# Decode block backward: the last head's two gradient stores, issued from SyncE in parts of 120 and 8 rows

## The chip, the cores and the metric

One NeuronCore of a Trainium2 chip runs the whole program. The metric is the device time of one execution in microseconds (us). Most of the program's data stay in HBM, and 16 DMA engines carry them to and from the on-chip memory. A DMA can be issued from SyncE (SP), from ScalarE (ACT) or from GpSimd (POOL); each of the three has a queue of its own in the profile (q1, q10 and q0).

## What is computed

The reference is the forward pass of a decode block (one new token, batch 2) and its gradients:

```python
h  = x + attention(layernorm(x), k_cache, v_cache, wq, wo)   # 32 heads, 4096 cached keys, 128 per head
h2 = h + relu(layernorm(h) @ w1) @ w2                        # width 640, hidden 1728
out0 = h2;  gradients for x, k_cache, v_cache, wq, wo, w1, w2 from grad_out
```

The two large outputs are the gradients of the caches, `out_2` (keys) and `out_3` (values), each 2 x 32 x 4096 x 128 in bf16. For each of the 64 pairs of batch and head they are outer products. With p the softmax row of 4096 numbers and d the output gradient of the head, the value gradient is p times d. The key gradient is a second row, the gradient of the scores, times the query. Each of the two is 1 MB per head, so 128 of the 362 MB that the program moves are these stores.

## The kernel before

A tile of a head is laid out with 128 partitions of 32 cache positions each: a partition's row is 32 x 128 bf16, 8 KB in one piece, both in HBM and on chip.

The program has two passes over the 64 heads. The first (`p1_iter`) loads a K and a V tile per head and makes the softmax rows and the attention output. The second (`p2_iter`, `p2_tail`) loads V a second time (tile `Wt`), forms the gradient of the scores on TensorE, and makes two tiles on VectorE:

- `gV`, at the end of `p2_iter(j)`: `outer_half` (line 832) twice, and in the last three heads four of the last columns by ScalarE instead (line 899); then the store to `out_3` from GpSimd's queue (line 900).
- `gK`, at the end of `p2_tail(j)`, which runs within the next head's `p2_iter(j + 1)`, or alone after the last head: `outer_half` twice, then the store to `out_2` from GpSimd's queue (line 851).

So GpSimd issues stores in turn, gK of one head and gV of the next. The last two of all are the gV and the gK of head number 63 (`NP1 - 1`, where `NP1` is 64). The `give` after each store hands the tile's buffer to whatever takes it next, which waits for the store by itself; after the last head nothing takes one.

The loops write out all instructions in order (the schedule is by hand). Background generators are woven in between: weight gradients with stores from ScalarE's queue (`outer_rows`, line 968), and the gradient of x. The latter ends with two stores of 5 rows of 256 bytes each, issued by SyncE (`store_row`, line 653), and `out_0` has gone out earlier by the same lines. SyncE issues all loads, too. In program order its last entries are the load of the last `Wt` tile and the two 5-row stores of the gradient of x; the two stores of the last head follow them in time.

At the program's end SyncE waits for all DMAs, one semaphore after another (line 1288), and then all engines meet twice.

Of the kernel before, what the change touches and what calls it, by code (L numbers as in the profile page):

```python
# [15 lines left out]
def kernel(  # L16
# [20 lines left out]
    nc = tc.nc  # L37
# [36 lines left out]
    def pst(shape, dtype, role, name):  # L74

        k = banks[role].pop(0)
        banks[role].append(k)
        return ps.tile(shape, dtype, tag=f"bank{k}", bufs=1, name=name)
# [11 lines left out]
    def take(tag, shape, name):  # L90
        assert free[tag] > 0, (tag, name)
        free[tag] -= 1
        k = homes[tag].pop(0)
        t = pools[k].tile(shape, BF16, tag=f"big{k}", bufs=1, name=name)
        home_of[id(t)] = (tag, k, t)
        return t
# [9 lines left out]
    def give(t, to=None):  # L106
        tag, k, _ = home_of.pop(id(t))
        to = to or goes_to(tag)
        owned[tag] -= 1
        owned[to] += 1  # L110
        free[to] += 1
        homes[to].append(k)
        given_at[k] = step[0]
# [288 lines left out]
    NP1 = len(pairs)  # L402
# [24 lines left out]
    def pair_transpose(nat, g, dve=False, busy=0):  # L427


        t_ps = pst([128, GT // 2, 128], FP32, "tps", "t_ps")  # L430
        warm(t_ps[:].rearrange("p j k -> p (j k)"), nat, g, busy)
        natf = nat[:].bitcast(FP32)
        for j in range(GT // 2):
            cc = (g * GT) // 2 + j
            nc.tensor.transpose(t_ps[:, j, :], natf[:, 2 * cc:2 * cc + 2, :].rearrange("p c k -> p (c k)"), ident_f[:])  # L435
        t_sb = mats.tile([128, GT // 2, 128], FP32, tag="XT", bufs=4, name="t_sb")
        if dve:
            nc.vector.tensor_copy(out=t_sb[:], in_=t_ps[:])  # L438
        else:
            nc.scalar.copy(out=t_sb[:], in_=t_ps[:])  # L440
        return t_sb

    def pair_matvec(dst, t_sb, g, vecs):
        v = t_sb[:].bitcast(BF16).rearrange("p j (k two) -> p j k two", two=2)
        for j in range(GT // 2):
            sc = g * GT + 2 * j
            for par in range(2):
                nc.tensor.matmul(dst[:, sc:sc + 2], lhsT=v[:, j, :, par], rhs=vecs[:, par, :],  # L448
                                 start=(par == 0), stop=(par == 1))

    def natural(cache, b, h):
        return cache[b, h].rearrange("(p sc) d -> p sc d", sc=NSC)
# [377 lines left out]
    def outer_half(dst, row, colp, k, n=HALF):  # L830
        sl = slice(k * HALF, k * HALF + n)
        nc.vector.tensor_tensor(  # L832
            out=pairs_view(dst[:, sl, :]),
            in0=row.rearrange("p (a two) -> p a two", two=2)[:, None, :, :].to_broadcast([128, n, 64, 2]),
            in1=colp[:, sl, None, :].to_broadcast([128, n, 64, 2]), op=ALU.mult)

    def p2_tail(j):

        p = S2[j]
        bp, hp = turns[j]  # L840
        pair_matvec(p["dp"], p.pop("T3"), 3, gom[:, bp, hp, :, :])
        gsp = small.tile([128, NSC, 2], BF16, tag="gsp", bufs=2, name="gsp")
        nc.vector.scalar_tensor_tensor(
            out=gsp[:], in0=p["dp"][:, :, None].to_broadcast([128, NSC, 2]), scalar=negdot[:, hp, bp:bp + 1],
            in1=P_bf[:, p_slot[(bp, hp)], :, None].to_broadcast([128, NSC, 2]), op0=ALU.add, op1=ALU.mult)
        yield
        gK = take("g", [128, NSC, 128], "gK")
        outer_half(gK, p["rb"][:, 128:256], gsp, 0)
        yield
        outer_half(gK, p["rb"][:, 128:256], gsp, 1)  # L850
        nc.gpsimd.dma_start(out=natural(out_2, bp, hp), in_=gK[:])  # L851
        give(gK)
        del S2[j]
        yield
# [3 lines left out]
    def p2_iter(j, nsb):  # L858

        tail = p2_tail(j - 1) if j - 1 in S2 and "T3" in S2[j - 1] else iter(())  # L860
        c = S2[j]
        next(tail, None)
        b, h = turns[j]
        go = gom[:, b, h, :, :]
        bank = pst([128, 512], FP32, "sps", "dp_ps")
        for k, col in enumerate((goc, qsc)):
            nc.tensor.matmul(bank[:, 128 + k * 128:256 + k * 128],  # L867
                             lhsT=col[:, h, b:b + 1].to_broadcast([128, 128]), rhs=ident_bf[:],
                             start=True, stop=True)
        c["dp"] = bank[:, 0:NSC]  # L870
        rb = mats.tile([128, 256], BF16, tag="rb", bufs=3, name="rb")
        nc.scalar.activation(out=rb[:], in_=bank[:, 128:384], func=ACT.Copy, scale=rt[:, b, h:h + 1])  # L872
        pp = small.tile([128, NSC, 2], BF16, tag="pp", bufs=2, name="pp")
        nc.gpsimd.tensor_copy(out=pp[:], in_=P_bf[:, p_slot[(b, h)], :, None].to_broadcast([128, NSC, 2]))
        if nsb:
            pf = small.tile([128, NSB], FP32, tag="pf", bufs=2, name="pf")
            nc.gpsimd.tensor_copy(out=pf[:, 0:nsb], in_=P_bf[:, p_slot[(b, h)], NSC - nsb:NSC])
        c.update(rb=rb, pp=pp)
        c["T0"] = pair_transpose(c["W"], 0)
        next(tail, None)  # L880
        yield
        for _ in tail:
            yield
        c["T1"] = pair_transpose(c["W"], 1)
        pair_matvec(c["dp"], c.pop("T0"), 0, go)
        yield
        c["T2"] = pair_transpose(c["W"], 2)
        pair_matvec(c["dp"], c.pop("T1"), 1, go)
        yield
        c["T3"] = pair_transpose(c["W"], 3)  # L890
        give(c["W"], "g" if j < H and j != 1 and owned["g"] < 3 else None)
        pair_matvec(c["dp"], c.pop("T2"), 2, go)
        gV = take("g", [128, NSC, 128], "gV")
        outer_half(gV, c["rb"][:, 0:128], c["pp"], 0)
        yield
        outer_half(gV, c["rb"][:, 0:128], c["pp"], 1, HALF - nsb)
        if nsb:
            for k in range(nsb):
                nc.scalar.activation(out=gV[:, NSC - nsb + k, :], in_=rb[:, 0:128], func=ACT.Copy, scale=pf[:, k:k + 1])
        nc.gpsimd.dma_start(out=natural(out_3, b, h), in_=gV[:])  # L900
        give(gV)
        yield

# [266 lines left out]
    for n, (i, j) in enumerate(plan):  # L1170
# [22 lines left out]
        if j is not None:  # L1193
            if j < NP1:
                bg_until(("go", *turns[j]))
            nsb = 0 if i is not None else NSB if j < H and fin is None else NSB // 2 if j >= NP1 - 3 else 0
            g2 = p2_iter(j, nsb) if j < NP1 else p2_tail(NP1 - 1)
        elif open_tail:
            g2 = p2_tail(open_tail[0])
# [93 lines left out]
```

## Time and profile before

| what | value |
|---|---|
| time, median of three runs | 898.54 us (893.46 to 898.84) |
| the profiled execution | 896.3 us, of which 894.4 us span |
| moved over DMA | 361.84 MB, mean 405 GB/s |
| TensorE busy, share of the span | 83% |
| VectorE busy | 77% |
| GpSimd's queue (q0) | 134.23 MB, 36.1% of 16 engines' time |
| SyncE's queue (q1) | 211.13 MB, 58.1% |
| last gV store issued / landed | 876.05 / 890.29 us |
| last gK store issued / landed | 878.33 / 892.72 us |

The span runs from the first to the last instruction of the program; the time contains it and some 2 us around it. Times of day in this text are microseconds from the span's start. A store is issued by an instruction of half a microsecond on its engine; its data move later, when the DMA engines get to it, and the last of its 16 landings (one per DMA engine) ends it.

### The profile page before, as it was taken

What the parts mean: (1) busy time and instruction counts of PE and PEld (TensorE: products, weight loads), DVE (VectorE), ACT (ScalarE), POOL (GpSimd) and SP (SyncE); (2) the same over time, 40 slices, a digit from 0 to 9 for tenths busy, and PEclk for the clock granted to TensorE, in tenths of its full rate; (3) what the DMA queues carried; (4) which work ended last, traced back from release to release, by engine and by line L of the source; (5) the groups of instructions that cost most, each with busy time, mean ns of one, the idle gap of its engine ahead of it and who ended that gap; (6) DMA issues with size and microseconds to landing.
All of it is one profiled execution on the core that took longest, in us unless ns stands there. A gap on an engine that the chain in (4) does not pass through costs nothing.

```text
span 894.4 us, 24636 instructions
## 1 busy us (share of the span) xinstructions
PE 740.6 (83%) x10145; PEld 622.7 (70%) x10145; DVE 688.1 (77%) x1283; ACT 469.5 (52%) x1184; POOL 198.6 (22%) x342
## 2 busy tenths in 40 slices
PE   4999899999998998897867887875698988858881
PEld 4887788888887887777757776764566765635570
DVE  2666778976888897796678897877988468898992
ACT  1344334443555665464545776553476666537751
POOL 1344434442210000000011231111222111111141
PEclk9999989999999999898995555555657566555655
DMA  9999999999979999999999999999999999999996
GB/s 377 420 412 403 409 407 418 411 414 410 356 299 366 422 422 424 422 422 423 414 382 390 416 416 418 414 412 422 398 394 423 426 421 424 423 426 424 423 423 256
DMA packets 56304, 361.84 MB, mean 405 GB/s; under 512 B 5696, under 2 KB 11904, under 8 KB 15488
## 3 DMA queue, kind: packets, MB, share of 16 engines
q1 hardware_dynamic: 34536, 211.13, 58.1%
q0 software_dynamic: 18432, 134.23, 36.1%
q10 hardware_dynamic: 3224, 14.92, 4.0%
q8 instruction: 80, 1.31, 0.6%
q14 instruction: 32, 0.26, 0.1%
HBM read 211.11 MB, written 149.13 MB: 403 GB/s over the span
## 4 chain that ended last, share of the span: by engine, by line
DMA 37%; PE 31%; DVE 19%; issue 6%; ACT 3%; POOL 1%; SPq 0%; POOLq 0%; DVEq 0%; ACTq 0%
DMA out_dram<-gK 16%; PE t_ps L435 13%; DMA Vt<-in_A_v_cache_dram 12%; PE m_ps L469 7%; DMA out_dram<-gV 5%; DVE gV L832 5%; DVE gK L832 4%; DVE rows L658 4%; PE s_ps L448 3%; DVE pk L476 3%; DMA wo_t<-in_A_wo_dram 2%; PE u_ps L498 2%; DMA Kt<-in_A_k_cache_dram 2%; PE dp_ps L448 2%; ACT t_sb L440 1%
## 5 line engine op out<-in xcount | busy, mean ns | idle before, releaser
L440 ACT COPY t_sb<-t_ps 128x512 f32<-128x512 f32 x479 | 272.6, 587 | 181.3 <-PE t_ps L435 177.0
L448 PEld LDWEIGHTS <-t_sb 128*128 128x128 bf16 x4096 | 169.7, 103 | 75.1 <-ACT t_sb L440 33.3
L435 PE MATMUL t_ps<-ident_f,Wt 128*128 128x128 f32 x832 | 200.0, 392 | 0.4 <-ACT t_sb L440 0.4
L476 DVE TENSOR_TENSOR pk<-Kt,ep 128x2048 bf16<-128x2048 bf16 x128 | 156.3, 1222 | 44.7 <-ACT ep L523 26.0
L469 PE MATMUL m_ps<-pk,Vt 128*128 128x129 bf16 x2048 | 175.8, 224 | 15.0 <-DMA Vt<-in_A_v_cache_dram 14.4
L832 DVE TENSOR_TENSOR gK<-rb,gsp 128x2048 bf16<-128x2048 bf16 x128 | 153.4, 1224 | 18.5 <-DMA out_dram<-gV 16.9
L832 DVE TENSOR_TENSOR gV<-rb,pp 128x2048 bf16<-128x2048 bf16 (+2 forms) x128 | 147.1, 1172 | 23.6 <-DMA out_dram<-gK 23.1
L435 PEld LDWEIGHTS t_ps<-ident_f,Wt 128*128 128x128 f32 x832 | 140.2, 204 | 32.1 <-issue 26.5
L435 PE MATMUL t_ps<-ident_f,Kt 128*128 128x128 f32 x1024 | 153.4, 285 | 3.7 <-DMA Kt<-in_A_k_cache_dram 3.5
L469 PEld LDWEIGHTS <-Vt 128*128 128x128 bf16 x2048 | 130.9, 100 | 18.1 <-DMA Vt<-in_A_v_cache_dram 16.1
L435 PEld LDWEIGHTS t_ps<-ident_f,Kt 128*128 128x128 f32 x1024 | 116.3, 148 | 5.1 <-issue 2.6
L486 POOL COPY pk<-ep 128x16 bf16<-128x16 bf16 x80 | 83.6, 1047 | 152.3 <-ACT ep L523 107.0
L448 PE MATMUL dp_ps<-gom,t_sb 128*128 128x2 bf16 x2048 | 96.0, 168 | 14.5 <-ACT t_sb L440 14.1
L900 POOL DMA_DIRECT2D out_dram<-gV x64 | 34.3, 536 | 317.7 <-DVE gV L832 115.6
L448 PE MATMUL s_ps<-gom,t_sb 128*128 128x2 bf16 x2048 | 80.2, 164 | 1.2 <-DVE t_sb L438 1.2
L851 POOL DMA_DIRECT2D out_dram<-gK x64 | 34.1, 533 | 200.3 <-DVE gK L832 149.6
L582 ACT CAST MT<-m_ps 128x128 bf16<-128x128 f32 x64 | 17.0, 266 | 116.3 <-PE m_ps L469 116.3
L965 ACT CAST ot<-o_ps 128x512 bf16<-128x512 f32 (+3 forms) x152 | 66.8, 494 | 8.9 <-DMA out_dram<-ot 7.3
L872 ACT ACTIVATE rb<-dp_ps,rt 128x256 bf16<-128x256 f32 x64 | 30.3, 474 | 45.5 <-PE dp_ps L867 43.2
L658 DVE CUSTOM_DVE_ANT_0 rows<-wo_t,rows 128x640 bf16<-128x640 bf16 x64 | 52.3, 818 | 0.2
L658 DVE CUSTOM_DVE_ANT_0 rows<-wqs,gqr 128x1024 bf16<-128x1024 bf16 x40 | 48.8, 1220 | 0.2
L658 DVE CUSTOM_DVE_ANT_0 rows<-w_t,rows 128x640 bf16<-128x640 bf16 (+2 forms) x58 | 45.9, 792 | 2.8 <-ACT rows L636 2.1
(194 smaller groups left out, 715.7 us busy)
## 6 DMA issues: line engine op xcount, KB each, us to landing
Kt<-in_A_k_cache_dram SPq DMA_DIRECT2D x64, 1024.0 KB, 16.5
Vt<-in_A_v_cache_dram SPq DMA_DIRECT2D x64, 1024.0 KB, 16.6
out_dram<-gV POOLq DMA_DIRECT2D x64, 1024.0 KB, 14.1
out_dram<-gK POOLq DMA_DIRECT2D x64, 1024.0 KB, 14.3
Wt<-in_A_v_cache_dram SPq DMA_DIRECT2D x52, 1024.0 KB, 11.4
out_dram<-ot ACTq DMA_DIRECT2D x6, 960.0 KB, 12.7
wq_t<-in_A_wq_dram SPq DMA_DIRECT2D x5, 1024.0 KB, 11.0
wqs<-in_A_wq_dram SPq DMA_DIRECT2D x5, 1024.0 KB, 22.2
```

What stands on the lines that cost most here:

```text
L435: nc.tensor.transpose(t_ps[:, j, :], natf[:, 2 * cc:2 * cc + 2, :].rearrange("p c k -> p (c k)"), ident_f[:])
L440: nc.scalar.copy(out=t_sb[:], in_=t_ps[:])
L448: nc.tensor.matmul(dst[:, sc:sc + 2], lhsT=v[:, j, :, par], rhs=vecs[:, par, :], start=(par == 0), stop=(par == 1))
L469: nc.tensor.matmul(r["m"][:, 0:129], lhsT=r["V"][:, sc, :], rhs=r["pk"][sc // HALF][:, sc % HALF, 0:129], start=(sc == 0), stop=(sc == NSC ...
L476: nc.vector.tensor_tensor(out=p["pk"][k][:, :, 0:128].rearrange("p s (a two) -> p s a two", two=2), in0=p["K"][:, sl, :].rearrange("p s (a ...
L486: nc.gpsimd.tensor_copy(out=col, in_=e)
L658: nc.vector.tensor_tensor_reduce(out=junk[0:kc, 0:width], in0=in0, in1=in1, scale=1.0, scalar=0.0, op0=ALU.mult, op1=ALU.add, accum_out=acc)
L832: nc.vector.tensor_tensor(out=pairs_view(dst[:, sl, :]), in0=row.rearrange("p (a two) -> p a two", two=2)[:, None, :, :].to_broadcast([128 ...
L851: nc.gpsimd.dma_start(out=natural(out_2, bp, hp), in_=gK[:])
L872: nc.scalar.activation(out=rb[:], in_=bank[:, 128:384], func=ACT.Copy, scale=rt[:, b, h:h + 1])
L900: nc.gpsimd.dma_start(out=natural(out_3, b, h), in_=gV[:])
L965: nc.scalar.copy(out=ot[0:P, k, n0:n0 + nn], in_=o_ps[0:P, 0:nn])
```

## The change

A new function `store` takes over both stores of the second pass. For all heads but the last it issues what was issued before, from GpSimd. For the last head it issues two DMAs from SyncE: rows 0 to 119, and rows 120 to 127. Data, layout, the order of the computation and all other DMAs stay as they are. SyncE's list of instructions gets four DMAs at its end, behind the two 5-row stores (gV 120, gV 8, gK 120, gK 8 rows); GpSimd's list loses its last two.

```diff
+    def store(dst, t, last):
+
+        if not last:
+            nc.gpsimd.dma_start(out=dst, in_=t[:])
+            return
+        for rows in (slice(0, 120), slice(120, 128)):
+            nc.sync.dma_start(out=dst[rows], in_=t[rows])
+
     def p2_tail(j):
...
         outer_half(gK, p["rb"][:, 128:256], gsp, 1)
-        nc.gpsimd.dma_start(out=natural(out_2, bp, hp), in_=gK[:])
+        store(natural(out_2, bp, hp), gK, j == NP1 - 1)
         give(gK)
...
-        nc.gpsimd.dma_start(out=natural(out_3, b, h), in_=gV[:])
+        store(natural(out_3, b, h), gV, j == NP1 - 1)
         give(gV)
```

## The prediction

> **What bounds the kernel now.** The edit sits in the last 20 us, so I read first what limits that stretch, in the view of windows. The columns after each window are its length, the busy time of the five engines, the granted TensorE clock, the mean busy share of the core's 16 DMA engines, and GB/s.
>
> ```profile
> core 0: us, PE busy (x) PEld busy (x) DVE busy (x) ACT busy (x) POOL busy (x), PEclk, DMA share, GB/s
> 840.00:860.00 20.00, 16.71 (x137) 12.17 (x137) 19.69 (x35) 11.19 (x23) 4.29 (x7) 0.50 1.02 424
> 876.00:884.00 8.00, 0.00 (x0) 0.00 (x0) 2.03 (x2) 0.00 (x0) 1.07 (x2) 0.50 1.00 419
> 884.00:886.00 2.00, 0.00 (x0) 0.00 (x0) 0.00 (x0) 0.00 (x0) 0.00 (x0) 0.50 0.54 229
> 886.00:888.00 2.00, 0.00 (x0) 0.00 (x0) 0.00 (x0) 0.00 (x0) 0.00 (x0) 0.50 0.17 70
> 888.00:890.00 2.00, 0.00 (x0) 0.00 (x0) 0.00 (x0) 0.00 (x0) 0.00 (x0) 0.50 0.08 33
> 890.00:892.00 2.00, 0.00 (x0) 0.00 (x0) 0.00 (x0) 0.00 (x0) 0.00 (x0) 0.50 0.07 29
> ```
>
> DMA is full while data are left, and compute is over at 878 us. Then the share falls to 0.07 and stays there: one engine of 16 is 0.0625. So for the last 4 us a single DMA engine works through what it still owes, and the kernel waits for it. Who waits shows in the timeline of POOL and SP and in SP's waits (waiter, what for, total us, times, longest):
>
> ```profile
> 873.70 0.53 POOL L851 DMA_DIRECT2D out_dram<-gK  x1 [0.25 <-DVE gK L832]
> 876.05 0.53 POOL L900 DMA_DIRECT2D out_dram<-gV  x1 [1.82 <-ACT gV L899]
> 878.33 0.53 POOL L851 DMA_DIRECT2D out_dram<-gK  x1 [1.75 <-DVE gK L832]
> ...
> 867.46 3.63 SPq L653 DMA_DIRECT2D out_dram<-rows  x2
> ...
> SPq L1288 <- DMA out_dram<-gV: 19.2, 1, 19.2
> SPq L1288 <- DMA out_dram<-gK: 2.4, 1, 2.4
> ```
>
> The two stores that the edit touches are issued at 876.05 and 878.33. SP has nothing after its second row store at 870.8, and waits at the program's end for exactly these two.
>
> The trace also has every landing (16 per full transfer, one per DMA engine) and every DMA packet (queue, start, duration, size, not which engine). The last gV store lands on fifteen engines from 881.2 to 886.25 and on the sixteenth at 890.29. The last gK store: fifteen by 888.70, the sixteenth at 892.72. The ten POOL stores before them show the same picture, a last landing 4.0 to 4.6 us after the second last. Meanwhile ACT's large stores land on all 16 within 0.0 to 0.4 us of the second last. So one engine is late by some 4 us in POOL's backlog, and the tail of the windows is that engine. One row of 8 KB costs an engine 0.306 us (packets of 0.309 us, each starting 0.003 us before its predecessor's end), so the eight rows that it has of a 128-row store take 2.45 us.
>
> **The change part by part.** *Taken away:* two issues of 0.53 us on POOL. They end at 876.58 and 878.86. The late engine then works on earlier stores until 887.39, and the engine that finishes first (883.29) is also still on earlier ones, until 878.38. Backlog hides the issue everywhere: saving it is worth 0, from 0 to 0.1.
>
> *Added:* four issues on SP, at 0.29 us (the row stores) to 0.37 us (a Wt load) each. They stand behind the two row stores of L653, the last of which issues at 870.8, before gV is complete at about 876. Both wait for the same DVE and ACT results as before. Nothing stands behind them but the program's end. gK's second part issues about 0.7 us after 878.3, still under the same backlog. Cost 0; without that cover it would be 0.4 to 0.7 us.
>
> *Moved:* 256 rows of 8 KB from queue q0 to q1. Bytes and time per packet stay: 840 to 860 us, with two queues mixed, ran at 424 GB/s against 419 with q0 alone. An engine that holds packets of two queues takes turns between them (in the trace, 256-byte packets of q1 stand between 8 KB packets of q0 without a gap). It then finishes when the sum of its work is done, whatever the order.
>
> What counts is therefore **how many rows the late engine gets**. Before it had 8 + 8. No DMA of 120 or of 8 rows is in the trace. The nearest are the 5-row stores of L653. I strung the packets on one engine together by their starts (a start 3 or 4 ns before the end of the packet ahead). For the last pair, issued at 867.46 and 870.80, the strings are clear: the five 256-byte packets of a store lie on five different engines, and the late engine is one of them. It carries a row at 871.11 and one at 874.40, in the string whose POOL stores complete at 872.42, 875.07, 877.57 and so on to 892.30. (For the pair issued near 800 the strings cross and I can't tell.) So small transfers are dealt row by row, and the late engine is among the first to get one. 120 rows go evenly onto 15 engines in eights. An engine that is served when only five are should be among the fifteen, and among the eight that take one row each of the 8-row part.
>
> That gives 9 + 9 rows, two more than before: 2 x 0.306 = **+0.61 us**. Bounds: 0 + 0 rows (left out of all four parts), at which the second-latest engine ends the kernel, -4.0 us; and 16 + 16 rows (the whole 8-row part on this one engine), +4.9 us. I take 9 + 9, since the 5-row stores are nearest. An end 0.3 us earlier is possible if POOL's last drain, which holds the end until 893.66 (SP is done at 893.36), has less to wait for; but q0's last rows on the late engine take turns with q1's, so I count 0.
>
> The Trainium skill's page "DMA: Bandwidth & Descriptors" (section "Why a DMA increments its semaphore by 16 and not by 1") says that SP's path takes the largest engine count up to 16 that divides the rows, lowest-numbered engines first: 15 for 120 rows, 8 for 8 rows, 5 for 5. By it the late engine, one of five, stays served by all four parts, and the sum would again be +0.61 us; the trace agrees for 5 rows (five packets on five engines), and shows neither 120 nor 8.
>
> Sum: 0 + 0 + 0 + 0.61 = +0.6 us. On the profiled execution (896.3 us, of which 894.4 are span) that is 896.9. The median of the runs is 898.54, 2.2 us above the profiled one, so on it the forecast is **899.1 us**, 0.07% more. About 1% (9 us) is what a measurement of this kernel can tell from no change, so this counts as none.
>
> **The rivals.** *The late engine is the one left out (faster).* If 120 rows go onto fifteen engines, one gets nothing, and if the 8 rows avoid it too, its 16 rows (4.9 us) are gone; it would end at 887.39. The kernel then ends with the second-latest engine, landing at 888.70, or 889.31 if that one gets two single rows: 3.4 to 4.0 us earlier, 894.5 to 895.1 on the median. For it: the tail is exactly one engine, and leaving out one engine is what a 120-row part can do. Against it: that engine took a row of both 5-row stores of the last pair. The same page (section "Latency and other measured facts") notes that engines 7 and 15 are usually the slow ones; if the late one were 15, this rival would hold, at the 894.5 to 895.1 just worked out. The trace bears out one clearly late engine but not its number.
>
> *The small part piles up (slower).* If a part's rows are dealt in blocks of eight, as the 120 are, the 8-row part lands whole on one engine. If that is the late one, it has 16 rows of each store instead of 8: 16 x 0.306 = 4.9 us more, 903.4 on the median. On any other engine it costs at most 4.9 - 4.0 = 0.9 us, since the second-latest has 4.0 us in hand. It decides only if block and late engine meet. Against it: the 5-row stores went onto five engines.
>
> *The late engine gets eights but no single rows:* 0 us, 898.5. This lies inside the forecast's own range.
>
> **How the numbers follow.** The forecast with the 0 us variant: 0.62. Late engine left out: 0.28. Pile-up: 0.10. The three runs spread from 893.46 to 898.84, wider than any of these effects. The forecast's own range is 896 to 900.5 (898.5 to 899.1, and half the spread of the runs downward, some 1.5 upward); the left-out case reaches down to 894.5, and a median that falls low to about 893. The pile-up, at 903 or more, is left outside. Range 893.2 to 900.8. All cases lie within 9 us of 898.5, so only scatter gives the outer classes: faster by over 1% 0.03 (from the left-out case), slower by over 1% 0.02 (from the pile-up), within 1% 0.95.
>
> **What would show it.** Right: the windows of the new profile end with a stretch of some 4 us at a share of 0.06 to 0.08, the last landings of the two 120-row parts are fifteen with one some 4 us behind, and each 8-row part has one late landing too. The SP rows show four issues at L843 of about 0.3 us, after the two row stores. POOL's last store is gK of the head before. Wrong in favour of the left-out case: the share falls from 0.5 to 0 within some 4 us with no one-engine tail, and the wait at the end is for an earlier POOL store or for an engine with little lag. Wrong in favour of the pile-up: the tail at one engine grows from about 4 to about 9 us. The forecast fails altogether if the wait before the end moves to SP's own issue, or if engines stand idle between 878 and 884, which would mean that backlog doesn't hide the four issues.

## The result, and the profile after

The changed kernel takes 898.62 us (median of 22 runs, 894.82 to 900.64). Beside it, the kernel before takes 896.34 us (22 runs, 893.46 to 899.05). The ratio is 1.002 with a 95% interval of 1.001 to 1.0029: about 1.8 us more (0.9 to 2.6). The forecast was 0.61 us more, so its direction holds and its size is too small. That the forecast time of 899.1 us lies so near the measured 898.62 is luck: it was added to the median of the first three runs of the kernel before (898.54), and added to the median of its 22 runs it would be 896.95, some 1.7 us too low.

The profiled execution of the changed kernel took 900.58 us, 898.8 of them span. It is some 4 us behind the one shown of before already ahead of the first change (the second row store is issued at 874.7 us and not at 870.8), which is scatter between executions. So times of day can't be set side by side, only distances. The view of windows at the end of the changed kernel:

```profile
core 0: us, PE busy (x) PEld busy (x) DVE busy (x) ACT busy (x) POOL busy (x), PEclk, DMA share, GB/s
880.00:882.00 2.00, 0.00 (x0) 0.00 (x0) 1.93 (x2) 0.00 (x0) 0.00 (x0) 0.50 1.05 426
882.00:884.00 2.00, 0.00 (x0) 0.00 (x0) 0.00 (x0) 0.00 (x0) 0.00 (x0) 0.50 1.00 299
884.00:886.00 2.00, 0.00 (x0) 0.00 (x0) 0.00 (x0) 0.00 (x0) 0.00 (x0) 0.50 0.90 287
886.00:888.00 2.00, 0.00 (x0) 0.00 (x0) 0.00 (x0) 0.00 (x0) 0.00 (x0) 0.50 0.92 307
888.00:890.00 2.00, 0.00 (x0) 0.00 (x0) 0.00 (x0) 0.00 (x0) 0.00 (x0) 0.50 0.67 254
890.00:892.00 2.00, 0.00 (x0) 0.00 (x0) 0.00 (x0) 0.00 (x0) 0.00 (x0) 0.50 0.26 107
892.00:894.00 2.00, 0.00 (x0) 0.00 (x0) 0.00 (x0) 0.00 (x0) 0.00 (x0) 0.50 0.11 45
894.00:896.00 2.00, 0.00 (x0) 0.00 (x0) 0.00 (x0) 0.00 (x0) 0.00 (x0) 0.50 0.07 29
896.00:898.80 2.80, 0.00 (x0) 0.00 (x0) 0.00 (x0) 0.00 (x0) 0.00 (x0) 0.50 0.01 6
```

Read the last two columns together. At 880 us a full share still moves 426 GB/s. From 882 the share is 1.00 and the rate is 299: the engines are as busy as before and move 30% less. The kernel before has no such rows; it goes from a share of 1.00 at 419 GB/s straight to idle engines. After that the old picture returns: a share of 0.07, one engine of sixteen, until the end. The four issues are in the timeline of SP, and their durations (least, median, most in ns) in the view of line 843:

```profile
871.39 3.63 SPq L653 DMA_DIRECT2D out_dram<-rows  x2
879.76 1.85 SPq L843 DMA_DIRECT2D out_dram<-gV  x2
881.96 3.77 SPq L843 DMA_DIRECT2D out_dram<-gK  x2
```

```profile
L843 SPq DMA_DIRECT2D out_dram<-gV x2: 329/900/1470, 879.8 to 880.1; - x2
L843 SPq DMA_DIRECT2D out_dram<-gK x2: 1737/1864/1992, 882.0 to 884.0; - x2
```

They stand behind the two row stores, as foreseen, but three of them last 1.5 to 2.0 us and not 0.3. In the timeline of POOL the last store is gK of the head before (first fence). SP's wait at the end lasts 11.4 us, from about 885.7, when its own last issue is over (second fence, from the view of waits):

```profile
877.63 0.53 POOL L840 DMA_DIRECT2D out_dram<-gK  x1 [0.25 <-DVE gK L832]
```

```profile
SPq L1296 <- DMA out_dram<-gK: 11.4, 1, 11.4
```

The packet records give the rest. A 120-row part has 15 landings and one early increment of its semaphore; an 8-row part has 8 landings, the other 8 increments coming at once. Strung together backwards from the last packet, the late engine has in each store eight rows of the 120-row part and one row of the 8-row part. From 888.92 to 896.82 it works without a gap and takes turns between the two queues; the eight rows of the large gK part start from 889.24 to 893.75, its row of the small part at 894.37, and the last packets are GpSimd's gK of the head before. Not all of its rows last 0.309 us: from 883.65 on they are 0.59 us longer in all, 0.34 of it in a single row of 0.651 us. And the 256 moved rows last 0.384 us on the mean: the median is still 0.309, but 15.6% take over 0.5 us, the longest 1.405. The last 512 rows of the program, taken alike in both kernels, last 0.312 us before and 0.363 after, which over 16 engines is 512 x 0.051 / 16 = 1.6 us.

### The profile page after: what moved, and what is told of

Its sections match the earlier page's. It is cut to its first block, busy times and chain, and to the rows that moved or that the text cites. A ratio compares the mean times of both kernels' runs of the same rounds, so it can differ in the third digit from the quotient of the medians.

```text
span 898.8 us, 24639 instructions
## 1 busy us (share of the span) xinstructions
PE 744.1 (83%) x10145; PEld 624.6 (69%) x10145; DVE 688.5 (77%) x1283; ACT 469.6 (52%) x1184; POOL 195.6 (22%) x340
## 4 chain that ended last, share of the span: by engine, by line
PE 38%; DMA 32%; DVE 18%; ACT 5%; issue 4%; SPq 1%; DVEq 0%; POOL 0%; ACTq 0%; POOLq 0%
PE t_ps L435 17%; DMA Vt<-in_A_v_cache_dram 12%; DMA out_dram<-gV 8%; PE m_ps L469 7%; DMA out_dram<-gK 5%; DVE gK L832 4%; DVE gV L832 4%; DVE rows L658 4%; PE s_ps L448 3%; DVE pk L476 3%; DMA wqs<-in_A_wq_dram 3%; PE o_ps L967 3%; DMA wo_t<-in_A_wo_dram 2%; ACT t_sb L440 2%; PE u_ps L498 2%
## 5 line engine op out<-in xcount | busy, mean ns | idle before, releaser
L435 PE MATMUL t_ps<-ident_f,Wt 128*128 128x128 f32 x832 | 203.3, 397 | 0.5 <-ACT t_sb L440 0.4
L435 PEld LDWEIGHTS t_ps<-ident_f,Wt 128*128 128x128 f32 x832 | 142.3, 207 | 32.5 <-issue 26.2
```

## The experiments

Two theories stood at first. *Rows*: the late engine has 9 + 9 rows and not 8 + 8, and each row more costs 0.306 us at the end. *Queue*: SyncE's queue, with its neighbours and its place, is what costs. Later a third came up, *dealing*: parts that don't have 128 rows are dealt to the engines in another way, in which the engines hold each other up. Edits are shown against the loop of the changed kernel, unless the text says otherwise. Ratios are to the kernel before, run beside it on the same chip.

**Whole stores from SyncE.** Only the queue changes, nothing is divided.

```diff
-        for rows in (slice(0, 120), slice(120, 128)):
-            nc.sync.dma_start(out=dst[rows], in_=t[rows])
+        nc.sync.dma_start(out=dst, in_=t[:])
```

> The last head's two stores go out from SyncE as before in the change, but whole: 128 rows in one DMA each. Theory A (what the change costs is the two extra rows on the late DMA engine, and slower packets because 120 rows are dealt to the engines in other eights than 128 rows): 8 + 8 rows on the late engine as before, packets of the two stores back at 0.31 us (0.384 us in the change), so the time is that of before within 0.5 us (ratio 1.000). Theory B (the cost is the queue: q1 beside q0 in the last 20 us slows packets): packets stay at 0.36 to 0.40 us, and 0.8 to 1.5 us of the cost stay (ratio 1.001 to 1.0015).

Measured: 896.05 against 896.92 us, ratio 0.9992 (0.9978 to 1.0006). The moved rows last 0.311 us. The issues in SP's timeline:

```profile
876.33 0.35 SPq L842 DMA_DIRECT2D out_dram<-gV  x1
878.79 0.35 SPq L842 DMA_DIRECT2D out_dram<-gK  x1
```

Both the slow rows and the long issues are gone. The queue alone costs nothing that can be measured; the division does.

**The same parts from GpSimd.** Only the division, on the old queue.

```diff
-            nc.sync.dma_start(out=dst[rows], in_=t[rows])
+            nc.gpsimd.dma_start(out=dst[rows], in_=t[rows])
```

> The same parts of 120 and of 8 rows, but issued from GpSimd, as the stores of all other heads. Theory A: if GpSimd deals as SyncE does, the late engine gets 9 + 9 rows and the packets are slow again, +0.6 to +1.8 us over before; if GpSimd deals the 8-row part to other engines than the late one, 8 + 8 rows and 0 to +1 us. Theory B (the queue): everything in one queue, packets at 0.31 us, at most +0.6 us.

Measured: 900.34 against 896.92 us, ratio 1.0039 (1.0024 to 1.0054), 3.5 us more (2.2 to 4.8). That is more than either theory allowed (1.8 us at most). GpSimd's rows in the last 20 us last 0.377 us on the mean. Two engines are late here, not one; the windows of its tail show two sixteenths:

```profile
888.00:890.00 2.00, 0.00 (x0) 0.00 (x0) 0.00 (x0) 0.00 (x0) 0.00 (x0) 0.50 0.15 57
890.00:892.00 2.00, 0.00 (x0) 0.00 (x0) 0.00 (x0) 0.00 (x0) 0.00 (x0) 0.50 0.13 49
892.00:894.00 2.00, 0.00 (x0) 0.00 (x0) 0.00 (x0) 0.00 (x0) 0.00 (x0) 0.50 0.11 45
```

So the slow rows aren't a matter of SyncE's queue, nor of its long issues: POOL issued each part in about half a microsecond. SyncE's queue may be the cheaper one for the divided stores; with one head the two intervals still touch (1.0010 to 1.0029 from SyncE). Why GpSimd's parts cost more than was expected stays open.

**Parts of 125 and 3 rows.** A strong dose of rows: 125 rows should go onto five engines, 25 on each.

```diff
-        for rows in (slice(0, 120), slice(120, 128)):
+        for rows in (slice(0, 125), slice(125, 128)):
```

> Parts of 125 and of 3 rows from SyncE. 125 rows should be dealt to five engines, 25 rows each, 3 rows to three. Theory A (the late engine is among the lowest-numbered five, whichever part is issued): the late engine gets 25 or 26 rows a store instead of 8, 34 to 36 more in all, x 0.306 = +10.4 to +11.0 us, and the tail of one engine lasts some 6 us longer than the other four that got as much. Rival (the late engine is not in the set that a part of 120 or 125 rows starts with): it loses its 16 rows and the five others gain 34 rows less their lead of 4 us: +6.4 us or less, and the five end together.

Measured: 906.25 us, ratio 1.0102 (1.0085 to 1.0118), 9.1 us more. The windows show five sixteenths (0.31) until the end nears, then the late ones:

```profile
886.00:888.00 2.00, 0.00 (x0) 0.00 (x0) 0.00 (x0) 0.00 (x0) 0.00 (x0) 0.50 0.31 127
...
894.00:896.00 2.00, 0.00 (x0) 0.00 (x0) 0.00 (x0) 0.00 (x0) 0.00 (x0) 0.50 0.31 127
...
900.00:902.00 2.00, 0.00 (x0) 0.00 (x0) 0.00 (x0) 0.00 (x0) 0.00 (x0) 0.50 0.09 37
```

The large gK part lands on five engines at 897.01, 897.53, 897.76, 901.06 and 902.58 us, and the last of the three single rows at 902.90. The engine that is late in GpSimd's backlog (its last row there lands at 894.38) is among the five: its 25 rows of the large gK part last until 901.06, and it has no single row. The engine that ends the kernel, with 25 + 1 rows, is the second-latest in GpSimd's backlog (892.03). So rows on the late engines do cost at the end. The forecast was 10.4 to 11.0 us, from 25 or 26 rows on the late engine; 9.1 us (7.6 to 10.6) reaches into it.

**Where the late engine stands.** The kernel before, with its last row stores divided (5 rows as 2 + 3, then as 4 + 1), so that each 256-byte packet marks an engine. The data stored are the same.

```diff
-    def store_row(col_bf, n, dst):
+    def store_row(col_bf, n, dst, first=0):
...
-        nc.sync.dma_start(out=dst, in_=r[0:n])
+        for rows in ([slice(0, first), slice(first, n)] if first else [slice(0, n)]):
+            nc.sync.dma_start(out=dst[rows], in_=r[rows])
...
-            store_row(gxo[:], ND, out_1[b].rearrange("s (c p) -> (s c) p", p=128))
+            store_row(gxo[:], ND, out_1[b].rearrange("s (c p) -> (s c) p", p=128), 2 + 2 * b)
```

> The kernel before, except that the two 5-row stores of the gradient of x go out in parts: 2 and 3 rows the first time, 4 and 1 the second. This marks the engines: the engine that is first in the dealing gets a 256-byte packet of the 2-row, of the 3-row and of the 4-row part; so does the second; the third only of the 3- and the 4-row part; the fourth of the 4-row part; the fifth of none. Where the late engine's string of packets carries them tells its place. No effect on the time is expected (two more issues of 0.3 us on SyncE that nothing waits for).

One execution, 896.0 us. The late engine is known by its landings, the last of each GpSimd store: 870.08, 872.70, 875.30, 877.84 us and so on. Its string of packets, followed along them from 869.56 to 892.07, carries none of the ten marks (870.10 to 875.39), so it isn't among the four engines that these parts used. **The same marks in the changed kernel:**

> The changed kernel with the marks of the run before (2 and 3 rows, then 4 and 1, instead of two times 5), to see in one run the late engine's place and how many rows of the four parts it gets: 9 + 9 if it is among the first eight, 8 + 8 if it is the ninth to fifteenth, 0 + 0 if it is the sixteenth, in which case the tail of one engine is missing and the end comes some 4 us earlier.

One execution, 894.9 us. Here, too, the late engine's string, followed along its landings (870.98, 873.66, 876.17, 878.65 us), carries none of the ten marks. So in both it comes behind the first four in the dealing, while in the kernel before it carries a row of both 5-row stores. The fifth place fits every execution that was read, the one with 125 rows included (one of five, with no row of the 3-row part); a place that changes from one execution to the next isn't shown. A division that gives less to that place wasn't tried.

For the tail I take the distance from the last landing of the gV store of head number 61, which all these kernels issue alike and ahead of the two stores in question, to the last landing of all: 12.21 us before, 12.21 in the marked kernel before, 12.18 with whole stores from SyncE, 13.01 in the changed kernel and 12.83 in the marked changed one. The strings say what it consists of. In the marked changed kernel the late engine has 9 + 9 rows, all of 0.309 to 0.313 us: the two extra rows alone, 0.61 us, as forecast. In the changed kernel it has 9 + 9 as well, but one of the 18 lies ahead of that landing; the distance grows by one row (0.31) and by the 0.59 us that its rows are longer. So there the late engine has 0.61 + 0.59 = 1.2 us more in all, and 0.6 in the marked one: between these two executions, what the slow rows cost differs by whether they fall on the late engine.

**Parts of 112 and 16 rows.** Each engine gets 7 + 1, no engine more than before. If the extra rows are all that costs, the cost is gone.

```diff
-        for rows in (slice(0, 120), slice(120, 128)):
+        for rows in (slice(0, 112), slice(112, 128)):
```

> The parts from SyncE are of 112 and of 16 rows. Both divide by 16, so every engine gets 7 + 1 rows of a store: the late engine has 8 + 8 as before, not 9 + 9. Theory 'rows' (the change's cost is the two extra rows on the late engine): ratio to before 1.000, packets don't matter. Theory 'dealing' (the cost is that parts other than 128 rows are dealt to the engines in pieces of adjacent partitions, so that two engines read through one port at once): packets of the two stores stay slow, 0.35 to 0.42 us on the mean with some near 0.61 (twice 0.306), and 0.5 to 2 us are left (ratio 1.0005 to 1.002).

Measured: 899.1 against 896.5 us, ratio 1.0026 (1.0008 to 1.0043). The cost stays with even rows, and the rows last 0.399 us. Its windows show full shares at falling rates, as in the changed kernel:

```profile
880.00:882.00 2.00, 0.00 (x0) 0.00 (x0) 0.00 (x0) 0.00 (x0) 0.00 (x0) 0.50 0.98 328
882.00:884.00 2.00, 0.00 (x0) 0.00 (x0) 0.00 (x0) 0.00 (x0) 0.00 (x0) 0.50 0.97 283
```

The tail of its profiled execution is the old 12.21 us, though; that execution, at 895.88 us, was the quickest of its twelve, and so shows where the cost isn't rather than where it is.

**Two halves of 64 rows.** As above, with `slice(0, 64), slice(64, 128)`.

> The parts from SyncE are of 64 and 64 rows, 4 rows for each engine, so again 8 + 8 rows a head's store on the late engine. Theory 'dealing': partitions 0 to 63 lie behind half of the ports, so all 16 engines read two to a port and packets go to 0.45 to 0.61 us on the mean while only one part is moving; +1.5 to +4.9 us (ratio 1.0015 to 1.0055). Theory 'rows': even dealing, 0.31 us packets, ratio 1.000.

Measured: 897.83 us, ratio 1.0015 (0.9999 to 1.0031): not told apart from none. The rows are the slowest of all at 0.433 us, 27% of them over 0.5 us. So for one head the cost isn't seen to grow with the mean row. The Trainium skill's page "DMA: Bandwidth & Descriptors" (section "Rules for kernel authors") advises against two transfers to disjoint halves of the partitions, because both go over the same engines. The trace agrees on the engines (16 landings for each half of gV), and adds that rows get slower on the mean.

**Six heads whole from SyncE.** For the lag of the late engine: if GpSimd's queue makes it, moving the last six heads off that queue should take it away. The condition becomes `j >= NP1 - 6`, the store is whole.

> The stores of the last six heads (twelve DMAs) go out whole from SyncE's queue, and only those before them from GpSimd's. Nothing else of SyncE's stands behind them but the four small row stores among them. Theory 'POOL' (the lag of 4 to 6 us of one engine is made by GpSimd's path, for SyncE's and ScalarE's transfers land on all engines within 0.4 us): the lag is not renewed over the last 45 us, the end comes 2 to 4 us earlier (ratio 0.9955 to 0.998). Theory 'engine' (the engine has that much more work, or loses time whatever the queue): the lag moves into SyncE's stores, ratio 1.000.

Measured: 895.99 us, ratio 0.9987 (0.9971 to 1.0003). Three engines now end last within 1.1 us of each other (893.21, 893.73 and 894.26), the other thirteen by 891.47. But the kernel isn't clearly faster, and the idle time has moved:

```profile
860.00:880.00 20.00, 12.12 (x118) 10.40 (x119) 13.74 (x25) 8.43 (x21) 1.73 (x4) 0.50 0.81 335
880.00:890.00 10.00, 3.39 (x44) 2.85 (x42) 6.91 (x7) 3.45 (x8) 0.00 (x0) 0.67 1.01 416
```

DVE is busy 13.74 of 20 us here against 17.85 in the kernel before, the DMA share falls to 0.81, and the last gK tile is done at 886.94 us and not at 878.03. So the lag is smaller at the end, and idle time stands ahead of it instead. Whether GpSimd's queue makes the lag isn't settled by this: three engines stay late in stores that all come from SyncE, but they may have brought that lag along from GpSimd's stores.

**Six heads in parts, and a control.** One head costs 0.2 to 0.3%, close to what can be told. Six should cost six times as much if the dealing is at fault. The control also divides each store in two on SyncE's queue, but by columns, so that every part has 128 rows (of 4 KB). Both keep the condition `j >= NP1 - 6`; the diff leads from the parts of 112 and 16 rows to the control.

```diff
-        for rows in (slice(0, 112), slice(112, 128)):
-            nc.sync.dma_start(out=dst[rows], in_=t[rows])
+        for c in (slice(0, 16), slice(16, 32)):
+            nc.sync.dma_start(out=dst[:, c], in_=t[:, c])
```

> The stores of the last six heads go out from SyncE, each in parts of 112 and 16 rows (8 rows for every engine). Against whole stores of six heads (0.9987 of before) this has the same rows per engine. Theory 'dealing': packets of these stores at 0.38 to 0.42 us instead of 0.31; 12 stores x 8 rows x 0.08 us = up to 7.7 us more for each engine, of which waits in the stretch hide some: +2 to +8 us against the whole stores (ratio to before 1.001 to 1.008), and more than the column halves of this call. Theory 'rows': no more than the column halves, both at 0.9987 to 1.000.

> The control for the last: the same number of DMAs of the last six heads from SyncE, but each part has all 128 rows and half of the columns (4 KB a row), so the rows are dealt as for whole stores. It carries what two DMAs a store cost by themselves (issues, a ring of eight semaphores, a packet more per row). Both theories: packets of 4 KB at 0.155 to 0.16 us, ratio 0.9985 to 1.001.

Measured: by rows 906.02 us against 897.36, ratio 1.0100 (1.0080 to 1.0121); by columns 895.9 us, ratio 0.9987 (0.9974 to 1.0000). This is the reading that decides. The window of 860 to 880 us, parts of rows first, halves of columns second:

```profile
860.00:880.00 20.00, 7.66 (x81) 6.13 (x79) 9.37 (x16) 4.93 (x11) 0.37 (x2) 0.59 0.91 276
```

```profile
860.00:880.00 20.00, 12.36 (x143) 10.47 (x142) 16.81 (x24) 10.58 (x25) 1.73 (x4) 0.59 0.92 370
```

From 860 to 880 us the engines are busy for the same share, 0.91 and 0.92, and move 276 and 370 GB/s. DVE does 9.37 us of work and 16.81. Its waits for buffers whose stores haven't landed yet (from the view of waits, 840 to 910 us: total us, times, longest) are 10.5 us by rows and 3.1 by columns:

```profile
DVE gV L832 <- DMA out_dram<-gK: 6.8, 1, 6.8
DVE gK L832 <- DMA out_dram<-gV: 3.7, 1, 3.7
```

```profile
DVE gV L832 <- DMA out_dram<-gK: 2.6, 1, 2.6
DVE gK L832 <- DMA out_dram<-gV: 0.5, 1, 0.5
```

The same in the queue totals (packets, MB, share of 16 engines' span), in the same order:

```profile
q1 hardware_dynamic: 36456, 223.71, 61.9%
```

```profile
q1 hardware_dynamic: 37992, 223.71, 61.6%
```

The same bytes take 0.619 x 905.3 = 560.4 us of the engines' time by rows and 0.616 x 894.0 = 550.7 by columns, 9.7 us more. The times differ by (1.0100 - 0.9987) x 897 = 10.1 us, or 1.7 us for each of the six heads. That is near what the change costs for its one head (1.8), but it comes by way of buffers that later tiles wait for, and after the last head nothing takes a buffer. So the two sizes need not have the same account.

**Six heads of 120 and 8.** The dealing and the extra rows together.

> The parts of the change, 120 and 8 rows, for the stores of the last six heads, from SyncE. Theory 'rows and dealing' together: as the 112 and 16 rows of this call, and on top 12 x 0.306 = 3.7 us for the first eight engines, which get 9 rows of each store: +0.2 to +0.4% over the 112 and 16 rows if the late engine is among the first eight, as it was where it could be told; 0 if not, and then the sixteenth engine has 96 rows less.

Measured: 906.49 us, ratio 1.0113 (1.0091 to 1.0134). It lies 0.0013 above the even parts, with intervals that overlap: what the uneven rows add over six heads can't be told from nothing here.

**Six heads of 112 and 16 from GpSimd.** The six heads of 112 and 16 rows again, with `nc.gpsimd` in the loop. From SyncE the issues had grown as well, to medians of 1.4 and 1.7 us where columns and whole stores take 0.33. GpSimd's issues don't grow.

> The stores of the last six heads in parts of 112 and 16 rows, as in the run before that cost 1.0% this way, but issued from GpSimd's queue. In that run SyncE's issues of the parts had also grown, to medians of 1.4 and 1.7 us (columns and whole stores: 0.33 us). Theory packets (the cost lies within the DMA engines, whoever issues): the moved rows again last 0.37 us or more on the mean instead of 0.311, and 1536 rows x 0.06 to 0.10 us / 16 engines = 6 to 10 us, a ratio of 1.006 to 1.012. Rival issue (the cost was SyncE's long issues, which brought the stores out late and with them the buffers that VectorE waits for): GpSimd issues in about 0.53 us and idles for most of this stretch, so the ratio goes back to between 0.998 and 1.003, whatever single packets last. A value between 1.003 and 1.006 would mean that both have a part.

Measured: 909.59 against 897.0 us, ratio 1.0149 (1.0126 to 1.0173). The issues (ns) and the same window:

```profile
L843 POOL DMA_DIRECT2D out_dram<-gV x12: 499/518/542, 847.8 to 888.2; - x12
L843 POOL DMA_DIRECT2D out_dram<-gK x12: 499/517/543, 852.8 to 892.4; - x12
```

```profile
860.00:880.00 20.00, 12.33 (x131) 10.29 (x129) 14.29 (x25) 9.29 (x21) 5.84 (x14) 0.59 0.91 283
```

The issues are short, the rows last 0.42 us (those from GpSimd between 860 and 880), and a share of 0.91 again moves only 283 GB/s. So SyncE's long issues aren't the cause. The 4.4 us above the same parts from SyncE ((1.0149 - 1.0100) x 897) fall outside the range that was expected. GpSimd here also waits 19.3 us in all for earlier stores to land before it issues (13.8 for gK, 5.5 for gV), which may be part of it; that wasn't tried by itself.

## Why the prediction was right, and where not

- *Issue on GpSimd, saved: 0.* Right, as far as it can be seen: whole stores from SyncE give 0.9992, an interval that holds 1.
- *Added: four issues of 0.29 to 0.37 us, hidden.* The size is wrong: 0.33, 1.47, 1.74 and 1.99 us. They cost nothing that can be seen: the last one ends at 885.7, 11 us ahead of the end, the DMA share is 0.90 or more to 888 us, and the same division from GpSimd, without long issues, costs no less.
- *Moved: "Bytes and time per packet stay".* This is the step that failed. The bytes stay, the time per row does not: 0.384 us instead of 0.309. Over 256 rows and 16 engines that is 256 x 0.075 / 16 = 1.2 us on the mean engine, a term that the sum has at 0. On the late engine, which sets the end, it was 0.59 us (GpSimd's rows included) in the profiled execution and nothing in the marked one. The rows of 424 and 419 GB/s that I argued from compare queues; they say nothing of parts with other than 128 rows. Of those the trace of before had the 5-row stores, and two loads and a store of 64 rows of 1280 bytes, which I had overlooked; the rows of that store last 55 ns on the mean, those of the 128-row store of the same width 56, so those small rows don't show it. The unknown cost was bounded by where rows go and not by how long they last.
- *9 + 9 rows on the late engine, +0.61 us.* Right, by the packets of both executions of the changed kernel that were read. The trace agrees here with the count of engines that the Trainium skill's page "DMA: Bandwidth & Descriptors" states (section "Why a DMA increments its semaphore by 16 and not by 1"): 15 landings for 120 rows, 8 for 8, five for 125. With both terms the late engine has 1.2 us more in the one execution and 0.6 in the other; the runs say 1.8 us (0.9 to 2.6), an interval that holds the first and not the second. The even parts of 112 and 16 cost 2.3 us (0.7 to 3.9) without any extra row.
- *The late engine left out (faster).* It wasn't, in either of the executions of the changed kernel that were read. The argument behind the chance, that the 5-row stores tell its place, held: in every execution read the place fits the fifth. The Trainium skill's page "DMA: Bandwidth & Descriptors" (section "Latency and other measured facts") names engines 7 and 15 as usually the slower ones. The traces number no engine; by the rule that the prediction cites, lowest-numbered engines first, one of the five that carry a 5-row store is neither of them, and the trace then disagrees.
- *The pile-up.* Ruled out: 8 landings for 8 rows.

**What stays open.** That parts by rows make the rows slow is shown on both queues, and that parts by columns don't, on SyncE's. Why is only argued. The Trainium skill's page "DMA: Bandwidth & Descriptors" (section "The descriptor swizzle") says that in a transfer to 128 partitions each engine writes one port of the on-chip memory; the stores here read that memory. If other parts were dealt in neighbouring partitions, several engines could meet at one port. That is a guess: no record here names partitions or ports, and another dealing also changes which addresses in HBM are written at the same time, which no run here separates. Also open is the rest of the 1.8 us for one head, of which 0.6 and 1.2 us can be seen on the late engine in the two executions that were read.

## What to carry to other kernels

If a store has to be divided, divide it along the row and keep all 128 partitions in each part: over six heads, halves of columns cost nothing here, parts of 112 and 16 rows some 1.7 us a head from SyncE. Read share and GB/s together: a full share at 280 instead of 420 GB/s means engines that are busy and slow, which no count of bytes or issues shows. Where one engine ends the kernel, follow that engine's own packets; a mean over all 16 doesn't tell when it is done. And before a sum puts "time per packet stays", look for a packet of the new shape in the trace, and give that term bounds if there is none.

## What the runs showed that I had not expected

- An 8 KB row lasts 0.309 us in a store of 128 rows, and on the mean 0.384 (120 + 8), 0.399 (112 + 16) and 0.433 us (64 + 64), with single ones of up to 1.4 in the changed kernel. On the late engine most rows still last 0.309 us.
- Large stores on SyncE are issued in 0.33 to 0.35 us (medians) when their parts have 128 rows. With other parts the issues last up to 3.1 us, the longest in the kernel with six heads of 120 and 8. On GpSimd each takes about 0.5 us, whole or in part.
- One engine ends some 4 us after the others in the kernel before. Its place in the dealing fits the fifth in every execution read (among the first five in two, not among the first four in two others).
